# Turning the direction in which three products of a fused attention, gated convolution and channel mix kernel read their columns

## The chip, the cores and the metric

The kernel runs on one core of a Trainium2 chip. The metric is the device time of one execution in microseconds (us), from the profiler's clock of the chip. Several runs of the kernel before were timed. One further execution was profiled instruction by instruction, and all rows below come from it. PE is the matmul engine (PEld its weight loads), DVE the vector engine, ACT the scalar engine, POOL GpSimd, SP the engine that issues DMAs.

## What is computed

Batch 8, 8 heads, 576 positions, head size 64, so x has 8 × 576 rows of 512. Three stages follow one another:

```python
# linear attention, with softmax over features (q) and over positions (k)
kv = np.einsum('bhsd,bhse->bhde', k_s, v)
x = np.einsum('bhsd,bhde->bhse', q_s, kv)          # -> (8, 576, 512)
# gated causal convolution of 5 taps
gate = 1.0 / (1.0 + np.exp(-gate_pre))
y = gate * (x @ w_val) @ w_out
# channel mix with the position before
xk = mu_k * y + (1.0 - mu_k) * y_prev
xr = mu_r * y + (1.0 - mu_r) * y_prev
k = np.maximum(xk @ w_k, 0.0)                       # 512 -> 1024
v = k * k @ w_v                                     # 1024 -> 512
out = 1.0 / (1.0 + np.exp(-(xr @ w_r))) * v
```

## The kernel before, in words

The 4608 rows are cut into twelve tiles of T = 384 positions. Each tile i goes through five dense products, each with a name in the trace: pv (W_val, steps V), py (W_out, steps Y), racc (W_r, steps R), ph (W_k, steps H) and vacc (W_v, steps A). In pv, py and ph the weights are the stationary operand (128 × 128) and the activations are the moving operand, 384 columns; the output bank holds features by positions. In racc and vacc a slice of 128 positions of the activations is stationary (`part`, line 621) and a weight row of 512 columns moves; the output bank holds positions by features.

The first tile multiplies plain fp32 operands, one matmul call for each pair of operands (`left` has one member). From the second tile on, weights and activations are each split into a high and a low part of the type fp32r, and a product takes three passes: high by high and the two mixed ones. Both cases run through one helper, `passes` (lines 445 to 451), whose matmul call is line 449. So line 449 stands for all five dense products and for px, the product of q with the key-value sums; the output's name tells them apart in the trace.

The order of work is written out by hand: the list `FRONT` (lines 22 to 37) for the first two tiles with the loading and splitting of the weights, then for each tile the steps V, Y, R and an alternation of H and A, with the list `REST` saying which side steps (the attention of the next tile, the gates, the mixes) come after which step. Each engine's queue runs in that order. [...] ACT and DVE empty a bank after the last matmul of its group.

The change touches `passes` and its two kinds of callers: `product` (line 568), which pv, py and ph use from the second tile on, and the steps `r` (line 624) and `vacc` (line 646). The first tile's pv and py go through `row` (line 572).

Of the kernel before, what the change touches and what calls it, by code (L numbers as in the profile page):

```python
# [66 lines left out]
def tile_linear_attention_gated_conv_channel_mix(  # L67
# [15 lines left out]
    nc = tc.nc  # L83
    B, H, S, D = q.shape
    DM = H * D
# [3 lines left out]
    P = 128  # L89
    NC = DM // P  # L90
    NF = DFF // P
# [97 lines left out]
    def tap(c, t):  # L189
# [6 lines left out]


    HALF = ("wout", "wv")
    SHAPES = {"wval": (w_val, DM, DM), "wout": (w_out, DM, DM), "wr": (w_r, DM, DM), "wk": (w_k, DM, DFF), "wv": (w_v, DFF, DM)}
    CHUNKS = {  # L200
        f"{w}{x}": (w, at) for w, (_, rows, width) in SHAPES.items()
        for x, at in enumerate((kc, c0) for c0 in range(0, width, WC) for kc in range(rows // P))
# [4 lines left out]
    def place(dtype, name):  # L207
        return wts.tile([P, WC], dtype, tag="w", bufs=PLACES, name=name)

    def load_weight(n):  # L210
        w, (kc, c0) = CHUNKS[n]
        here = n in LEFT_WEIGHTS
        raw = raws[n] = (first if here else early).tile([P, WC, 2], U32, tag="raw", bufs=1 if here else 6, name="raw")
        nc.sync.dma_start(raw.rearrange("p n w -> p (n w)"), SHAPES[w][0][kc * P:(kc + 1) * P, 2 * c0:2 * (c0 + WC)])

# [5 lines left out]
    def open_upper():  # L221
        pool = ctx.enter_context(tc.tile_pool(name="upper", bufs=1))
        for w in ("wk", "wv"):
            _, rows, width = SHAPES[w]
            t = pool.tile([P, rows // P, width], F32R, name=f"{w}_hi")
            upper.update({(w, kc): t[:, kc, :] for kc in range(rows // P)})

    def split_weight(n):
# [9 lines left out]
        l = lower[at] = place(F32R, "lower")  # L238
        scale = 0.5 if w in HALF else 1.0
        nc.scalar.activation(h, t, AF.Copy, scale=scale)  # L240
        nc.vector.scalar_tensor_tensor(out=l, in0=t, scalar=scale, in1=f32(h), op0=ALU.mult, op1=ALU.subtract)

    def weight(i, w, kc, c0, n):

        at = w, (kc, c0 // WC * WC)
        o = c0 % WC
        if i == 0:
            return (whole[at][:, o:o + n],)
        return upper[w, kc][:, c0:c0 + n], lower[at][:, o:o + n]
# [192 lines left out]
        nc.vector.tensor_sub(pair[1], a, f32(pair[0]))  # L442
        return pair

    def passes(po, left, right, start, stop, turn=False):

        m = ((0, 0),) if len(left) == 1 else ((0, 0), (0, 1), (1, 0)) if turn else ((0, 0), (1, 0), (0, 1))
        for x, (a, b) in enumerate(m):
            nc.tensor.matmul(  # L449
                po, lhsT=left[a], rhs=right[b], start=start and x == 0, stop=stop and x == len(m) - 1  # L450
            )

    def padded(i, h, tag, bufs, name, pool=odd):

# [41 lines left out]
    def x_chunk(st, i, c):  # L496
        segs = segments(i)
        g = len(segs)
        px = ps_w.tile([P, 512], F32, tag="w", name="px")
        for o, n, b, s in segs:  # L500
            kv = (kvf[b],) if i < 2 else kvs[b % 2]
            passes(px[:, o:o + n], tuple(a[:, c, :] for a in kv), tuple(a[:, o:o + n] for a in st["q", c]), True, True)
        xv = padded(i, HALO, "xf", 2, "xf") if i else padded(i, HALO, "xf", NC, "xf", first)
        data = xv[:, :, HALO:]
        fill_past(i, xv, tail_x[:, c, :])
        nc.scalar.copy(data, px[:, :T].rearrange("p (g t) -> p g t", g=g))
        keep_tail(i, xv, tail_x[:, c, :])
        st["xv", c] = xv
        if i == 0:
            st["x", c] = (xv[:, 0, HALO:],)  # L510
            return
        xh, xl = st["x", c] = x_pair("x")
        gx = lambda a: a.rearrange("p (g t) -> p g t", g=g)
        nc.scalar.copy(gx(xh), data)
        nc.vector.tensor_sub(gx(xl), data, gx(f32(xh)))
# [38 lines left out]
    def main_steps(i, xs):  # L554
# [3 lines left out]
        st = {}  # L558
        gx = lambda a: a.rearrange("p (g t) -> p g t", g=g_n)

        def bank(pool, tag, name):
            return pool.tile([P, 512], F32, tag=tag, name=name)
# [4 lines left out]

        def product(po, w, at, acts):
            for c, a in enumerate(acts):
                passes(po, weight(i, w, c, at, P), a, c == 0, c == NC - 1)  # L570

        def row(po, w, c, a):

            for m in range(NC):
                passes(po[m][:, :T], weight(i, w, c, m * P, P), a, c == 0, c == NC - 1)

        def val(m):
            if i == 0:
                if m == 0:
                    st["pv"] = four("pv")  # L580
                row(st["pv"], "wval", m, xs["x", m])
                return
            pv = bank(ps_w, "w", "pv")
            product(pv[:, :T], "wval", m * P, [xs["x", c] for c in range(NC)])
            gated(m, pv)
# [8 lines left out]
        def y(c):  # L594
            if i == 0:
                if c == 0:
                    st["py"] = [bank(ps_w, "w", "py") if m < 2 else bank(ps_acc, "acc", "py") for m in range(NC)]
                row(st["py"], "wout", c, st["g", c])
                return
            py = bank(ps_w, "w", "py")  # L600
            product(py[:, :T], "wout", c * P, [st["g", m] for m in range(NC)])
            keep_y(c, py)
# [18 lines left out]
        def part(pair, t):  # L621
            return tuple(a[:, t * P:(t + 1) * P] for a in pair)

        def r(c):
            if c == 0:
                st["r"] = [bank(ps_acc, "acc", f"racc{t}") for t in range(NT)]
            for t in range(NT):
                passes(st["r"][t], part(st["xr", c], t), weight(i, "wr", c, 0, DM), c == 0, c == NC - 1, True)

        def rsig():  # L630
            for t in range(NT):
# [6 lines left out]
        def hid(f):  # L638
            ph = bank(ps_w, "w", "ph")
            product(ph[:, :T], "wk", f * P, [st["xk", c] for c in range(NC)])  # L640
            rf = one("k", 8, "rf") if i == 0 else scratch("rf")
            nc.scalar.activation(rf, ph[:, :T], AF.Relu)  # L642
            nc.scalar.activation(rf, rf, AF.Square)
            st["k", f] = (rf,) if i == 0 else split(rf, k_pair("k"))

        def vacc(fs, ts):

            if fs[0] == 0:
                st["v"] = [bank(ps_acc, "acc", f"vacc{t}") for t in range(NT)]
            for f in fs:  # L650
                for t in ts:
                    passes(st["v"][t], part(st["k", f], t), weight(i, "wv", f, 0, DM), f == 0, f == NF - 1, True)
            if fs[-1] == NF - 1 and len(ts) == NT:
                for t in ts:
                    finish(t)

        def finish(t):
            rs = st["rs", t]
            nc.vector.scalar_tensor_tensor(
                out=rs, in0=rs, scalar=1.0 if i else 0.0, in1=st["v"][t], op0=ALU.add, op1=ALU.mult  # L660
            )
            r0 = i * T + t * P
            nc.sync.dma_start(out[r0:r0 + P, :], rs)

        def last(t):

            vacc(range(NF - NT, NF), [t])
            finish(t)
# [6 lines left out]
        else:  # L675
            d += [("Z", t) for t in range(NT)]
        names = [("V", m) for m in range(NC)] + [("Y", c) for c in range(NC)] + [("R", c) for c in range(NC)] + d
        fns = {"V": val, "Y": y, "R": r, "H": hid, "A": lambda f: vacc([f], range(NT)), "Z": last}
        steps = {f"{n}{x}": lambda n=n, x=x: fns[n](x) for n, x in names}
        side = {"rsig": rsig}  # L680
# [127 lines left out]
```

## Time and profile before

| | |
|---|---|
| median of three runs | 812.14 us (810.77 to 812.4) |
| span of the profiled execution | 810.1 us |
| instructions in it | 12242 |
| PE busy | 798.3 us, 4578 matmul records |
| PEld busy | 701.2 us, 4578 weight loads |
| DVE busy | 564.5 us |
| ACT busy | 479.3 us |
| POOL busy | 59.2 us |
| DMA | 53.25 MB, mean 66 GB/s |

The span runs from the first instruction to the last; what lies around it makes up the rest of the time of a run. [...] A plain fp32 matmul leaves two records, an fp32r matmul one. The trace shows both types as f32; where the names hold `whole` the operands are plain fp32, where they hold `_hi`, `lower` or end in h or l they are fp32r.

### The profile page before, as it was taken

To read this page: it belongs to the slowest core of one execution; us is meant where nothing else is said; L and a number is where in the kernel's file an instruction comes from. 1 tells how busy PE (TensorE), PEld (TensorE's weight loads), DVE (VectorE), ACT (ScalarE), POOL (GpSimd) and SP (SyncE) were. 2 spreads that over 40 slices of the span, in tenths; PEclk is the share of its full clock that TensorE was granted. 3 is DMA by queue.
4 is the path that set the end of the run, shared out by engine and by line. 5 is a ranking of instruction groups with operands and counts; after the bars stand their busy time and mean duration, and the time that the engine had idled before them with its cause. 6 is when DMAs were issued, how large, how long until landed. Compare 5 with 4: busy or idle time off the path is not lost.

```text
span 810.1 us, 12242 instructions
## 1 busy us (share of the span) xinstructions
PE 798.3 (99%) x4578; PEld 701.2 (87%) x4578; DVE 564.5 (70%) x1016; ACT 479.3 (59%) x948; POOL 59.2 (7%) x224
## 2 busy tenths in 40 slices
PE   6999999999999999999999999999999999999998
PEld 5545588999999999989989999999999999998996
DVE  7999889976777577577758577577576747644611
ACT  4667678637746746655754763763764674664542
POOL 2130001000002001000000100100000100100000
PEclk9999999999999999999999999999999999999999
DMA  9786220132222102013041211211222010000001
GB/s 310 244 269 217 59 78 1 40 98 59 75 63 59 40 27 72 7 36 91 7 98 46 53 40 39 60 39 40 59 65 73 1 37 23 22 1 14 26 1 40
DMA packets 92537, 53.25 MB, mean 66 GB/s; under 512 B 74018, under 2 KB 84286, under 8 KB 92478
## 3 DMA queue, kind: packets, MB, share of 16 engines
q1 hardware_dynamic: 92432, 52.44, 22.3%
q8 instruction: 36, 0.59, 0.3%
q14 instruction: 23, 0.19, 0.1%
q10 hardware_dynamic: 46, 0.02, 0.0%
HBM read 43.02 MB, written 9.44 MB: 65 GB/s over the span
## 4 chain that ended last, share of the span: by engine, by line
PE 95%; DMA 2%; DVE 1%; ACT 1%; SPq 1%; issue 0%; ACTq 0%
PE ph L449 25%; PE vacc L449 25%; PE racc L449 12%; PE pv L449 12%; PE py L449 12%; PE px L449 4%; PE kvacc L347 2%; PE pq L476 2%; DMA raw<-in_moe_w_val_dram 1%; DMA raw<-in_moe_w_k_dram 1%; DVE gate L548 1%; DMA kt<-in_k_dram 1%; PE mx L333 0%; PE pmT L321 0%; SPq L303 0%; DVE whole L152 0%
## 5 line engine op out<-in xcount | busy, mean ns | idle before, releaser
L548 DVE SCALAR_TENSOR_TENSOR gate<-xf,cw,gate 128x384 f32<-128x384 f32 x192 | 117.2, 615 | 5.1 <-ACT gate L546 2.3
L449 PE MATMUL ph<-xkh,wk_hi 128*128 128x384 f32 x352 | 120.3, 342 | 0.0
L449 PE MATMUL ph<-xkl,wk_hi 128*128 128x384 f32 x352 | 118.3, 336 | 0.0
L449 PE MATMUL ph<-xkh,lower 128*128 128x384 f32 x352 | 118.1, 336 | 0.0
L642 ACT ACTIVATE rf<-ph 128x384 f32<-128x384 f32 x96 | 46.8, 488 | 99.0 <-PE ph L449 98.1
L449 PE MATMUL vacc<-wv_hi,kh 128*128 128x512 f32 x264 | 104.0, 394 | 0.0
L449 PE MATMUL vacc<-lower,kh 128*128 128x512 f32 x264 | 103.2, 391 | 0.0
L449 PE MATMUL vacc<-wv_hi,kl 128*128 128x512 f32 x264 | 103.1, 391 | 0.0
L442 DVE TENSOR_TENSOR kl<-rf,kh 128x384 fp32r<-128x384 f32 x88 | 48.9, 556 | 70.1 <-ACT kh L441 69.1
L616 DVE SCALAR_TENSOR_TENSOR xm<-yf,mus,xm 128x384 f32<-128x384 f32 x96 | 56.5, 614 | 24.2 <-ACT xm L615 23.7
L449 PEld LDWEIGHTS ph<-xkh,wk_hi 128*128 128x128 f32 x352 | 66.2, 188 | 2.0 <-ACT xkh L441 0.2
L449 PEld LDWEIGHTS ph<-xkh,lower 128*128 128x128 f32 x352 | 66.2, 188 | 1.9
L449 PEld LDWEIGHTS ph<-xkl,wk_hi 128*128 128x128 f32 x352 | 66.1, 188 | 0.0
L494 DVE TENSOR_TENSOR ql<-pq,qh 128x384 fp32r<-128x384 f32 x40 | 22.2, 556 | 62.5 <-ACT qh L493 62.5
L441 ACT CAST gh<-gf 128x384 fp32r<-128x384 f32 x44 | 22.5, 511 | 72.0 <-DVE gf L589 72.0
L449 PE MATMUL py<-gh,wout_hi 128*128 128x384 f32 x176 | 59.6, 343 | 0.0
L449 PE MATMUL pv<-xh,lower 128*128 128x384 f32 x176 | 59.5, 338 | 0.0
L449 PE MATMUL pv<-xh,wval_hi 128*128 128x384 f32 x176 | 59.5, 338 | 0.0
L449 PE MATMUL pv<-xl,wval_hi 128*128 128x384 f32 x176 | 59.3, 337 | 0.0
L449 PEld LDWEIGHTS vacc<-wv_hi,kl 128*128 128x128 f32 x264 | 49.5, 188 | 11.0 <-DVE kl L442 0.3
L449 PE MATMUL py<-gl,wout_hi 128*128 128x384 f32 x176 | 58.2, 339 | 0.0
L449 PE MATMUL py<-gh,lower 128*128 128x384 f32 x176 | 58.0, 338 | 0.0
(132 smaller groups left out, 1723.0 us busy)
## 6 DMA issues: line engine op xcount, KB each, us to landing
out_dram<-rs SPq DMA_DIRECT2D x36, 256.0 KB, 2.0
kt<-in_k_dram SPq DMA_DIRECT2D x16, 512.0 KB, 4.5
qt<-in_q_dram SPq DMA_DIRECT2D x29, 256.0 KB, 3.4
vt<-in_v_dram SPq DMA_DIRECT2D x56, 128.0 KB, 3.6
raw<-in_moe_w_k_dram SPq DMA_DIRECT2D x8, 512.0 KB, 5.5
raw<-in_moe_w_v_dram SPq DMA_DIRECT2D x8, 512.0 KB, 6.8
raw<-in_moe_w_val_dram SPq DMA_DIRECT2D x4, 512.0 KB, 6.3
raw<-in_moe_w_out_dram SPq DMA_DIRECT2D x4, 512.0 KB, 8.4
```

The source lines that it names most:

```text
L347: nc.tensor.matmul(acc[e * D:(e + 1) * D, x * VW:(x + 1) * VW], lhsT=kt[:, 2 * x + e, s, :], rhs=st["v"][:, 2 * x + e, s, :], start=(s == ...
L441: nc.scalar.copy(pair[0], a)
L442: nc.vector.tensor_sub(pair[1], a, f32(pair[0]))
L449: nc.tensor.matmul(po, lhsT=left[a], rhs=right[b], start=start and x == 0, stop=stop and x == len(m) - 1)
L476: nc.tensor.transpose(pq[:, t * P:(t + 1) * P], qt[:, t, 2 * c:2 * c + 2, :].rearrange("p h d -> p (h d)"), f32(ident))
L494: nc.vector.tensor_sub(ql, pq[:, :T], f32(qh))
L548: nc.vector.scalar_tensor_tensor(out=gx(gate), in0=xv[:, :, HALO - sh:HALO - sh + L], scalar=tap(c, HALO - sh), in1=gx(gate), op0=ALU.mult ...
L616: nc.vector.scalar_tensor_tensor(out=gx(xf), in0=yv[:, :, 1:], scalar=mu[:, c:c + 1], in1=gx(xf), op0=ALU.mult, op1=ALU.add)
L642: nc.scalar.activation(rf, ph[:, :T], AF.Relu)
```

## The change

Where a product is listed in `BACK`, the moving operand and the output of its matmuls are both given as views with the last dimension turned round (`[:, ::-1]`). That is W_val, W_r and W_k, wherever the operands come in two parts; with one part (the first tile) nothing changes. The stationary operand is given as before. The call for W_v carries the new argument too, but W_v isn't listed.

```diff
     HALF = ("wout", "wv")
+    BACK = ("wval", "wr", "wk")
...
-    def passes(po, left, right, start, stop, turn=False):
+    def passes(po, left, right, start, stop, turn=False, back=False):
 
         m = ((0, 0),) if len(left) == 1 else ((0, 0), (0, 1), (1, 0)) if turn else ((0, 0), (1, 0), (0, 1))
+        back = back and len(left) > 1
+        o = po[:, ::-1] if back else po
         for x, (a, b) in enumerate(m):
-            nc.tensor.matmul(
-                po, lhsT=left[a], rhs=right[b], start=start and x == 0, stop=stop and x == len(m) - 1
-            )
+            r = right[b][:, ::-1] if back else right[b]
+            nc.tensor.matmul(o, lhsT=left[a], rhs=r, start=start and x == 0, stop=stop and x == len(m) - 1)
...
-                passes(po, weight(i, w, c, at, P), a, c == 0, c == NC - 1)
+                passes(po, weight(i, w, c, at, P), a, c == 0, c == NC - 1, back=w in BACK)
...
-                passes(st["r"][t], part(st["xr", c], t), weight(i, "wr", c, 0, DM), c == 0, c == NC - 1, True)
+                passes(st["r"][t], part(st["xr", c], t), weight(i, "wr", c, 0, DM), c == 0, c == NC - 1, True, "wr" in BACK)
...
-                    passes(st["v"][t], part(st["k", f], t), weight(i, "wv", f, 0, DM), f == 0, f == NF - 1, True)
+                    passes(st["v"][t], part(st["k", f], t), weight(i, "wv", f, 0, DM), f == 0, f == NF - 1, True, "wv" in BACK)
```

## Rows read from the trace of the kernel before

**Rows 1.** The page's totals: engine, busy us, share of the span, instructions.

```profile
PE 798.3 (99%) x4578; PEld 701.2 (87%) x4578; DVE 564.5 (70%) x1016; ACT 479.3 (59%) x948; POOL 59.2 (7%) x224
```

**Rows 2.** The page's 40 equal slices, PE's busy tenths and granted clock's.

```profile
PE   6999999999999999999999999999999999999998
...
PEclk9999999999999999999999999999999999999999
```

**Rows 3.** The page's chain that ended last, by engine and by line.

```profile
PE 95%; DMA 2%; DVE 1%; ACT 1%; SPq 1%; issue 0%; ACTq 0%
PE ph L449 25%; PE vacc L449 25%; PE racc L449 12%; PE pv L449 12%; PE py L449 12%; PE px L449 4%; PE kvacc L347 2%; PE pq L476 2%; DMA raw<-in_moe_w_val_dram 1%; DMA raw<-in_moe_w_k_dram 1%; DVE gate L548 1%; DMA kt<-in_k_dram 1%; PE mx L333 0%; PE pmT L321 0%; SPq L303 0%; DVE whole L152 0%
```

**Rows 4.** Waits of PE: for whom, us in total, times, longest us.

```profile
PE heat L738 <- DVE ident L158: 3.3, 1, 3.3
PE pmT L321 <- DVE pm L314: 2.5, 1, 2.5
PE racc L449 <- ACT yf L607: 0.7, 1, 0.7
PE pq L476 <- ACT q L488: 0.7, 1, 0.7
PE pmT L321 <- ACT q L488: 0.6, 1, 0.6
PE px L449 <- ACT q L488: 0.2, 1, 0.2
```

**Rows 5.** Timeline inside one ph group: start us, us, engine, line, what.

```profile
407.47 0.34 PE L449 MATMUL ph<-xkh,lower 128*128 128x384 f32 x1
407.47 0.19 PEld L449 LDWEIGHTS ph<-xkl,wk_hi 128*128 128x128 f32 x1
407.64 0.34 PE L449 MATMUL ph<-xkl,wk_hi 128*128 128x384 f32 x1
407.65 0.19 PEld L449 LDWEIGHTS ph<-xkh,wk_hi 128*128 128x128 f32 x1
407.82 0.34 PE L449 MATMUL ph<-xkh,wk_hi 128*128 128x384 f32 x1
```

**Rows 6.** Pieces of the chain in order of time, fp32r: start us, us, matmuls.

```profile
198.32 2.08 PE ph L449 x12
...
747.97 8.34 PE pv L449 x48
...
764.78 8.17 PE racc L449 x36
```

**Rows 7.** Pieces of the same chain in the first tile, plain fp32.

```profile
81.40 2.58 PE ph L449 x8
85.78 2.58 PE vacc L449 x6
```

**Rows 8.** Groups by shape, PE, one pass of each: count, busy us, mean ns.

```profile
L449 PE MATMUL ph<-xkh,wk_hi 128*128 128x384 f32 x352 | 120.3, 342 | 0.0
...
L449 PE MATMUL pv<-xh,wval_hi 128*128 128x384 f32 x176 | 59.5, 338 | 0.0
...
L449 PE MATMUL racc<-wr_hi,xrh 128*128 128x512 f32 x132 | 51.4, 389 | 0.0
```

**Rows 9.** Groups by shape, weight loads: fp32, a plain run, one column repeated.

```profile
L449 PEld LDWEIGHTS ph<-xm,whole 128*128 128x128 f32 x64 | 11.9, 190 | 8.5 <-issue 1.9
...
L321 PEld LDWEIGHTS pmT<-ident,pm 128*128 128x128 f32 x32 | 4.3, 140 | 4.8 <-DVE pm L314 2.7 <-ACT q L488 0.8 <-issue 0.7
L333 PEld LDWEIGHTS mx<-ident,m 128*128 128x128 f32 x32 | 4.2, 141 | 2.1 <-DVE m L323 1.2
```

**Rows 10.** Groups by shape, ACT: copies out of PSUM, plain and in steps.

```profile
L486 ACT COPY q<-pq 128x384 f32<-128x384 f32 x4 | 1.9, 481 | 1.1 <-PE pq L476 1.1
L488 ACT COPY q<-pq 128x384 f32<-128x384 f32 x4 | 1.8, 475 | 2.4 <-PE pq L476 2.4
```

## The prediction

> **What bounds the kernel now.** I read the views in this order: the page's totals, its slices, the chain, the waits of the matmul engine, then single matmuls. The totals [rows 1] give PE 798.3 us of a span of 810.1, DVE 564.5, ACT 479.3. A busy PE alone proves little, since a matmul's record overlaps the next one's. [...] The chain that ended last [rows 3] is 95% PE, and nearly all of it is line 449, the one matmul call in `passes`: ph 25%, racc 12% and pv 12% belong to the products that are changed, vacc 25% and py 12% to those that are not. PE's waits are 8.0 us in six pieces [rows 4], the two longest 3.3 and 2.5 us, and none is in a product that is changed, except 0.7 us in the first tile's racc, which the change leaves alone. So what a matmul of line 449 costs more or less lands in the time one for one, as long as PE stays the engine that is late.
>
> What one matmul costs is read from the distance between starts, not from its record. The record of a 384-column matmul lasts 0.34 us, but the next starts 0.17 or 0.18 us later [rows 5]. The pieces of the chain give it exactly [rows 6]: 48 of pv in 8.34 us, 173.8 ns each; 12 of ph in 2.08 us, 173.3; 36 of racc in 8.17 us, 226.9. The two widths split this into a part per column and a fixed part. [...] The first tile multiplies in plain fp32, with two records per matmul, and there the chain [rows 7] shows 8 of ph in 2.58 us, 322.5 ns each, and 6 of vacc at 512 columns in 2.58 us, 430: 107.5 ns per 128 columns, 0.84 ns each, and nothing left over as a fixed part. [...]
>
> **The change part by part.** First, how many matmuls turn around. `back` is dropped where `left` has one member, and that is the first tile. Of the others the groups by shape [rows 8] hold 176 of pv, 352 of ph and 132 of racc for one of three passes, and the other two passes have as many: 528 + 1056 = 1584 at 384 columns and 396 at 512, 1980 in all. At today's distances they take 1584 × 173.5 = 274.8 us and 396 × 226.9 = 89.9 us, 364.7 us together, 45% of the span. py, vacc, px, the transposes and all of the first tile run as before.
>
> Second, what is not touched. No instruction is added or taken away, no tile is larger, no DMA moves, nothing passes a queue. The weight loads read `left`, which isn't turned. Each output element lands at its old address, because operand and output are turned alike: column 383 is read first and written to place 383. ACT and DVE read the bank after the last matmul of the group, so they wait for the same event as now. A column's sum is added up in the same order of passes. No wait is added and no buffer comes free at another point of the order.
>
> Third, the one thing that is touched: the step along the columns is −1 in SBUF and in PSUM. No matmul of the trace reads or writes so, and its price has to be bounded. For the cost per column one end is zero: the same columns, still neighbours. The far end is the slower of the rates that the engine shows, the first tile's: 322.5 instead of 173.5 ns at 384 columns and 430 instead of 226.9 at 512, so 1584 × 149.0 = 236.0 us and 396 × 203.1 = 80.4 us, together 316 us. [...] The fixed part can go both ways: at best it vanishes, as in the fp32 rows, −1980 × 13.3 ns = −26.3 us; as the other end I take that it doubles, +26.3 us.
>
> Which end is nearer? Three rows show an access that isn't a plain ascending run from an even place, and in none is it dearer. The weight load of mx reads one column over and over (step 0, from `to_broadcast` in line 333) and takes 141 ns, that of pmT reads 128 columns in a row and takes 140 [rows 9]. ACT's copy out of the bank in line 488 reads in steps of 128 places (the `rearrange` there) and takes 475 ns, the plain copy in line 486 takes 481 [rows 10]. [...] I take zero for both parts, and keep both ends.
>
> [...]
>
> **The sum.** The profiled execution: 810.1 us, +0 per column, +0 fixed, 810.1 us after. The median of the runs shown is 812.14 us, 2.0 us above that span, which lies around it and isn't touched. Forecast: 812.1 us, no change. The zero isn't hidden behind other work: PE is the path, so any nanosecond per matmul would show, 2.0 us for each. DVE at 564.5 us and ACT at 479.3 have room on either side: neither becomes the bound if PE lost 26 us, and if PE took longer their work would only be covered better.
>
> **The rivals.**
> - *Half rate.* [...] Time: 812.1 + 316 = 1128 us, and 1150 if the fixed 13.3 ns come on top (1980 × 11 to 13 ns). [...] Chance 0.20. [...]
> - *A dearer start.* A matmul that begins at the far end pays more before its first column or after its last. Price up to 13.3 ns each, as above: 812.1 to 838 us, with the middle at 825. It decides from 0.8 ns per matmul (1.6 us over 1980). For it: the fixed 13.3 ns exist and no row tells what they are. Against it: they are alike at 384 and 512 columns and in pv, ph and racc, though these read from quite different tiles. Chance 0.14.
> - *A cheaper start.* The fixed part is a meeting of the next weight load and the moving columns, both read upward now; the loads start with the matmul before them and last 0.19 us [rows 5], so the two do run side by side. Turning one of them might spare some of it, at most 26.3 us: 786 to 812 us. Against it: a load as long, 190 ns [rows 9], stands beside the fp32 matmuls, where nothing is left over, and the distance is the same for all weights. Chance 0.13.
> - *It doesn't do what it says*: the turned view is made into a plain one when the program is built. Then the times are those of no change; it is counted there, with 0.03.
>
> **How the numbers follow.** No change 0.53 (with the 0.03 above), half rate 0.20, dearer start 0.14, cheaper start 0.13. A measurement of this kernel can tell about 0.2% (1.6 us) from no change, so faster is 0.13, same 0.53, slower 0.20 + 0.14 = 0.34. The range that leaves out the half rate alone holds 0.80: from 812.1 − 26.3 = 786 to 812.1 + 26.3 = 838 us. The likeliest case's own range is 810.5 to 813.8.
>
> **What would show it.** If I'm right, 48 of pv still take 8.3 us in the chain, 36 of racc 8.2 and 12 of ph 2.1, and the span stays at 810. At half rate, the starts of turned matmuls stand 0.32 us (384) and 0.43 us (512) apart while py and vacc keep 0.17 and 0.23. If only the start is dearer or cheaper, pv and racc change by the same nanoseconds at both widths. If pv and ph change and racc doesn't, it hangs on what is read (activations there, weights in racc), not on the step as such. The forecast is wrong if any distance between starts moves by over 0.8 ns on the mean of the 1980, or if py or vacc move though they weren't edited.

## The result: 820.8 us, 1.07% slower, with the profile after

The changed kernel takes 820.84 us (median, 819.93 to 821.29) beside 812.25 us of the kernel before: a ratio of 1.0107, 95% interval 1.0093 to 1.0122. The time lies inside the range, but the forecast was no change, and the kernel is slower by 8.6 us, with an interval that leaves no change far outside.

The page's totals and chain of the changed kernel answer to [rows 1] and [rows 3]. Line 449 is line 453 now.

```profile
PE 806.1 (99%) x4578; PEld 706.3 (86%) x4578; DVE 565.2 (69%) x1016; ACT 479.8 (59%) x948; POOL 59.2 (7%) x224
...
PEclk9999999999999999999999999999999999999999
...
PE ph L453 25%; PE vacc L453 25%; PE racc L453 12%; PE pv L453 12%; PE py L453 11%; PE px L453 3%; PE kvacc L348 3%; PE pq L478 2%; DMA raw<-in_moe_w_k_dram 1%; DVE gate L550 1%; PE heat L740 1%; PE pmT L322 1%; PE mx L334 0%; DVE whole L152 0%; DVE raw L151 0%; DVE gf L591 0%
```

PE has 7.8 us more of busy time and as many records, DVE and ACT have what they had, and the granted clock is as in [rows 2], 9 tenths or more in all slices, 0.997 in the mean before and 1.000 after. The five products make up 85% of the chain, 86 before, and no other entry moves by more than 1%. The span is 817.9 us, 7.8 above that of before. The pieces of the chain (start us, us, what) that answer to [rows 6] and [rows 7] say where the time went:

```profile
81.05 2.58 PE ph L453 x8
85.42 2.58 PE vacc L453 x6
...
138.26 2.12 PE ph L453 x12
...
692.58 8.53 PE pv L453 x48
701.11 8.47 PE py L453 x48
709.58 8.40 PE racc L453 x36
...
748.17 4.12 PE vacc L453 x18
```

The last of these answers to this piece of the kernel before:

```profile
741.27 4.09 PE vacc L449 x18
```

A matmul of pv takes 8.53 / 48 = 177.7 ns in place of 173.8, of ph 176.7 in place of 173.3, of racc 233.3 in place of 226.9. The pieces of ph are short, so 0.01 us in one of them is 0.8 ns; the mean over all distances inside groups of ph in the two traces is 176.5 in place of 173.4. Adding up the time from each start to the next over the whole trace, by product, gives 3.1 us more in ph, 2.0 in pv and 2.4 in racc, 7.5 together. py, which wasn't turned, keeps its 8.47 us, and the plain fp32 matmuls of the first tile keep theirs. But vacc, which wasn't turned either, does not stay as it was: its mean distance rises from 228.8 to 230.0 ns, 1.0 us over its 792 matmuls. With 0.6 us less in py and px and small changes elsewhere, the sum over PE is 7.7 us, beside 7.8 in the span.

### The profile page after: what moved, and what is told of

The parts are those of the page before. It is cut to its first block, busy times and chain, and to the rows that moved or that the text cites. A ratio compares the mean times of both kernels' runs of the same rounds, so it can differ in the third digit from the quotient of the medians.

```text
span 817.9 us, 12248 instructions
## 1 busy us (share of the span) xinstructions
PE 806.1 (99%) x4578; PEld 706.3 (86%) x4578; DVE 565.2 (69%) x1016; ACT 479.8 (59%) x948; POOL 59.2 (7%) x224
## 4 chain that ended last, share of the span: by engine, by line
PE 96%; DVE 1%; DMA 1%; ACT 1%; issue 0%; ACTq 0%
PE ph L453 25%; PE vacc L453 25%; PE racc L453 12%; PE pv L453 12%; PE py L453 11%; PE px L453 3%; PE kvacc L348 3%; PE pq L478 2%; DMA raw<-in_moe_w_k_dram 1%; DVE gate L550 1%; PE heat L740 1%; PE pmT L322 1%; PE mx L334 0%; DVE whole L152 0%; DVE raw L151 0%; DVE gf L591 0%
```

## Experiments

Each kernel is compared with the kernel before, run beside it on the same chip. The kernels that hold many forms at once, called ladders below, ran once each and are read from their traces. "Distance" is the time from one matmul's start to the next one's. Most views are the same kind of row: the 36 matmuls of racc in one tile as a piece of the chain, which took 8.17 us before (226.9 ns each) and 8.40 after (233.3).

### Reading or writing: e1 and e2

e1 keeps the downward read and writes upward:

```diff
-            o = po[:, ::-1] if back else po
+            o = po
```

e2 keeps the downward write and reads upward:

```diff
-            r = right[b][:, ::-1] if back else right[b]
+            r = right[b]
```

> The moving operand of pv, ph and racc is read from the last column to the first, and the output is written upward, so the columns of these products come out mirrored and the kernel computes something else; counts and shapes are those of the changed kernel. Theory A (the price is in reading downward): the time of the changed kernel, 820.8 us, with mean distances of 177.8 ns in pv, 176.7 in ph and 233.4 in racc. Theory B (the price is in writing downward): the time of the kernel before, 812.2 us, with 173.5, 173.3 and 226.9 ns. Theory C (each side pays a part): between, and this run and the next add up to 8.6 us.

> The other half: operand read upward, output of pv, ph and racc written downward, again with mirrored columns. Theory A (reading): 812.2 us and the distances of the kernel before. Theory B (writing): 820.8 us and 177.8, 176.7 and 233.4 ns. Theory C: the rest of the 8.6 us.

Reading downward and writing upward: 820.77 us, ratio 1.0104 (1.0087 to 1.0121). Reading upward and writing downward: 812.28 us, ratio 0.9998 (0.9988 to 1.0007). One tile of each, e1 first:

```profile
692.92 8.53 PE pv L453 x48
701.45 8.47 PE py L453 x48
709.92 8.40 PE racc L453 x36
```

```profile
686.79 8.32 PE pv L453 x48
695.11 8.47 PE py L453 x48
703.58 8.17 PE racc L453 x36
```

Theory A holds: the pieces are those of the changed kernel in e1 and those of the kernel before in e2. The whole price is in reading the moving operand downward; writing to PSUM downward cost nothing.

### One pass alone, and all products: e3 and e4

e3 turns the second pass of three alone:

```diff
+            down = back and x == 1
+            o = po[:, ::-1] if down else po
+            r = right[b][:, ::-1] if down else right[b]
```

e4 turns all five products:

```diff
-    BACK = ("wval", "wr", "wk")
+    BACK = ("wval", "wout", "wr", "wk", "wv")
```

> Operand and output are turned in the second of the three passes alone, so the sums are those of the reference. Theory D (a fixed price for each downward matmul, wherever it stands): a third of the 8.6 us, 815.1 us, and the extra nanoseconds sit at the middle pass. Theory E (what counts is where one matmul ends and the next begins: up then down starts at the column just left): the price at the two turns differs from that of down after down; under 812.2 us if a turn spares the jump back to the other end of the row, over 820.8 us if adding to a column that was written a moment ago has to wait.

> W_out and W_v are turned as well. Theory D (fixed price by product shape): py has the shape of pv and ph and should gain 3.3 to 4.3 ns on 528 matmuls, 1.7 to 2.3 us, and vacc the shape of racc, 6.5 ns on 792, 5.1 us: 827.6 to 828.2 us. Theory F (the price comes of two directions next to each other, since py and vacc stay upward between the turned products): with one direction throughout it goes away, and the time is 812.2 us or near it.

e3 takes 818.46 us (1.0061 to 1.0091): a third of the matmuls, three quarters of the price. Neither theory gave that. In racc a piece of 36 takes 8.25 us, a third of the way from 8.17 to 8.40, as a fixed price would have it; in pv the 48 take 8.48, most of the way from 8.34 to 8.53, and in ph the mean distance is 176.5 ns, as with all three passes down. vacc, which isn't turned, rises to 230.9 ns. e4 takes 824.77 us (1.0134 to 1.0164), 3.9 us above the changed kernel where theory D wanted 6.8 to 7.4 and theory F a fall. The 48 of py rise from 8.47 to 8.59 us, 2.5 ns each, and vacc's mean distance from 230.0 in the changed kernel (228.8 before) to 233.4 ns. vacc had less to lose: it stood above 226.9 already. So there is no fixed price per downward matmul; what one pays depends on the matmuls around it, and matmuls that aren't turned can pay too.

### Ladders of widths, passes and starts: e5, e6 and e8

From here on one kernel holds many forms: a table `HOW` says for each product and tile how `passes` slices and turns, and the trace is read tile by tile. Shown is the core of e5.

```diff
         for x, (a, b) in enumerate(m):
-            nc.tensor.matmul(
-                po, lhsT=left[a], rhs=right[b], start=start and x == 0, stop=stop and x == len(m) - 1
-            )
+            first, end = start and x == 0, stop and x == len(m) - 1
+            l, r, o = left[a], right[b], po
+            if how and not first and not end:
+                lo, hi, down, held = how
+                l, r, o = l[:, 0:held], r[:, lo:hi], o[0:held, lo:hi]
+                if down:
+                    r, o = r[:, ::-1], o[:, ::-1]
+            nc.tensor.matmul(o, lhsT=l, rhs=r, start=first, stop=end)
```

e6 turns only the passes that `HOW` lists, in the first tile too; e8 is e5 with other columns and an output written upward.

> A ladder in one kernel: each tile of 384 positions runs racc, pv and ph in another form, so one trace holds all. racc: tile 2 down at 512 columns, 3 and 4 up and down at 384, 5 and 6 at 256, 7 up over columns 2 to 511, 8 down over 0 to 509, 9 and 10 up and down with 64 stationary columns, 11 down at 448. pv: tile 2 down at 384, 3 and 4 up and down at 320, 5 and 6 at 256, 7 and 8 with 64 stationary columns, 9 and 10 down and up at 352, 11 down over 0 to 381. ph: tile 2 down at 384, 3 and 4 down and up at 368, 5 down at 380, 6 at 376, 7 and 8 up and down over 16 to 383, 9 up from 2, 10 up from 14, 11 down over 0 to 381. The first and last matmul of each group stay whole and upward; parts of the products are left out. What counts are distances between starts, down minus up. Theory G (a fixed price at the start of a downward read): racc plus 6.4 ns at all widths, pv plus 4. Theory H (a price per column): racc plus 6.4, 5.6, 4.8 and 3.2 ns at 512, 448, 384, 256, pv from 4.1 at 384 to 2.7 at 256. Theory I (moving columns and weight load get in each other's way): with 64 stationary columns upward 512 takes 220 ns in place of 226.9, and the price of down falls to about 3. Theory J (what counts is the address on which a read begins): upward reads from 2 or 14 pay as the downward ones do, and downward ones from 510, 380, 376 or 368 differ from those from 384 or 512.

> A second ladder, operand and output turned alike, so the sums stay those of the reference. In pv, racc and ph, by tile: 0 all downward in plain fp32; 2 downward in the first and third pass; 3 none; 4 first pass alone; 5 second alone; 6 third alone; 7 first and second; 8 every other matmul; 9 all; 10 second and third. Theory D (a fixed price for each downward matmul): three distances of racc take 680.5 ns with none, plus 6.4 for each downward pass, and pv and ph 521 ns plus 3.3 to 4.3 for each. Theory E (turns matter): what a pass costs depends on its neighbours; by the run with the middle pass alone pv would take 529 with one downward pass, and the first or third pass alone would give the same 529; every other matmul would cost nearly as much as all. For tile 0: if the price is a wait in a stream that has no slack, fp32 at half the rate has slack and keeps 322.5 ns at 384 and 430 at 512 columns; if it is a start that nothing hides, 326 to 329 and 436.

> One width, other starting columns. racc with 448 columns: upward from column 0 (tile 1), 2, 4, 8, 16 and 32 (tiles 2 to 6), downward over the 448 columns from column 0, 2, 4, 8 and 16 (tiles 7 to 11). ph the same with 352 columns. pv by width, up and down: 368 (tiles 2, 3), 336, 304, 288, 272 (tiles 10, 11). The other columns are left out except in the first and last matmul of a group. Theory K (pieces of 16 columns): upward from 16 and 32 as from 0, 200.0 ns in racc; upward from 2, 4 and 8 dearer by the price of one more piece or by that of all pieces; downward from 16 as from 0, 205 ns. Theory M (start address alone): each start has its own price, upward and downward, with no order. The law of the first ladder, 0.026 ns for each column beyond 256, gives pv down minus up 2.9 ns at 368, 2.1 at 336, 1.2 at 304, 0.8 at 288 and 0.4 at 272.

Mean distances in ns, up and down, worked out from the starts in the traces, between matmuls of the same width (e5, where marked e8; whole rows upward from the kernel before for racc and from tile 1 of e5 for pv):

| read | up | down |
|---|---|---|
| racc, 512 columns | 227.0 | 233.6 |
| racc, columns 2 to 511 up, 0 to 509 down | 234.2 | 233.4 |
| racc, 448 columns (e8) | 203.5 | 205.9 |
| racc, 384 | 174.0 | 177.1 |
| racc, 256 | 119.4 | 118.1 |
| racc, 512, 64 columns held | 230.1 | 233.4 |
| pv, 384 | 173.6 | 177.5 |
| pv, 368 (e8) | 166.8 | 167.5 |
| pv, 336 (e8) | 154.8 | 153.1 |
| pv, 304 (e8) | 138.2 | 139.9 |
| pv, 256 | 118.5 | 118.1 |
| pv, 384, 64 columns held | 172.9 | 175.9 |

After e5 alone a law offered itself, 0.026 ns for each column beyond 256. e8 was its test, and it fell: 2.9, 2.1 and 1.2 ns were to stand between up and down at 368, 336 and 304 columns, measured were 0.7, −1.7 and 1.7. An upward read isn't always where a line through the whole rows of [rows 6] puts it either, 0.417 ns per column ((226.9 − 173.5) / 128) and 13.3 ns more: the first 384 columns of racc come near it, 174.0 for 173.5, but 448 columns would take 200 ns and take 203.5 from column 0, 206.2 from 2, 202.3 from 4, 205.5 from 8, 200.8 from 16 and 203.1 from 32. Theories G and H fail at 256 and 336 columns, where down isn't the dearer one; theory J fails in ph, where 382 columns from column 2 upward take 173.6 ns and 382 downward 176.9. What the ladder leaves is that width and start count for an upward read too: in racc one that begins two columns later takes 234.2 ns, where that line gives 226.1 for 510 columns, and so pays as much as a downward one.

Theory I is half borne out. Holding 64 columns shortens the record of a weight load from 188 to 134 ns, but an upward matmul of racc doesn't come down to 220 ns, it takes 230.1. What turning costs does fall, to 3.3 ns in racc and 3.0 in pv, near the 3 that was expected, though in racc only because the upward read got dearer. Groups by shape of e5's loads (count, busy us, mean ns):

```profile
L488 PEld LDWEIGHTS racc<-wr_hi,xrh 128*128 128x128 f32 x114 | 21.4, 188 | 3.0 <-ACT xrh L473 0.3
...
L488 PEld LDWEIGHTS racc<-wr_hi,xrh 128*64 128x64 f32 x18 | 2.4, 134 | 1.6
```

e6 answers two questions. Its first tile turns plain fp32, and the pieces of the chain show ph as in [rows 7]; racc of tiles 2 to 5, 9 and 11 follow (first and third pass down, none, first alone, second alone; all; none):

```profile
81.34 2.58 PE ph L488 x8
...
190.13 8.39 PE racc L488 x36
255.95 8.17 PE racc L488 x36
320.12 8.32 PE racc L488 x36
384.18 8.25 PE racc L488 x36
...
644.37 8.40 PE racc L488 x36
...
769.41 8.17 PE racc L488 x36
```

In plain fp32, at 322.5 / 384 = 0.84 ns per column and record, reading downward costs nothing: 322.5 ns. And one downward pass of three costs 0.15 us of the 0.23 if it is the first, 0.08 if it is the second, and 0.20 if it is the third (8.37 us); the first two together, at 8.45 us, cost more than all three. The neighbours count, as e3 said.

### Which step downward costs: e7 and e9

```diff
+    def read(a, how):
+
+        lo, hi, block, outer, inner = how
+        a = a[:, lo:hi]
+        if block:
+            a = a.rearrange("p (a b) -> p a b", b=block)
+            a = a[:, ::-1, :] if outer else a
+            return a[:, :, ::-1] if inner else a
+        return a[:, ::-1] if inner else a
```

e9 adds "every h-th group" and "swapped pairs" to it by a `rearrange` with three factors.

> The row is cut into blocks and only the order of the read is changed, the output is written upward, so columns come out permuted. Counted in racc (512 columns), pv and ph (384). Tile 2 all downward; 3 to 7: blocks taken from the last to the first, upward inside, with blocks of half the row, 64, 16, 4 and 2 columns; 8 to 11: blocks taken upward, downward inside, with blocks of 16, 4, 64 and half the row. The first and last matmul of each group stay upward and whole. [...] Theory K (a read is done in pieces of some columns, and what costs is the step from a piece to the one below): blocks of half the row cost nothing, blocks of 64 a fourth of the price or less, blocks of 16 and smaller the price of all downward, and blocks taken upward with downward reads inside 16 or 4 cost nothing. Theory L (what costs is each step of -1, wherever it is): blocks of 16, 4 and 2 taken down, upward inside, cost less the larger they are, and 16 or 4 downward inside cost as all downward. Theory M (what counts is only at which address a read begins and ends): half the row swapped already costs 6.6 ns in racc.

> A third ladder of read orders, racc with 512 columns, pv and ph with 384, output written upward, so columns come out permuted. Tiles 2, 3, 4: blocks of 8, 32 and 128 columns taken downward, upward inside; 5, 6, 7: blocks of 8, 32 and 128 taken upward, downward inside; 8 and 9: every second group of 4 or of 16 columns, then the others; 10: every fourth group of 4; 11: groups of 4 swapped in pairs. [...] Theory N (what counts is that the next group of 4 isn't the one above): every second group, every fourth group and swapped pairs cost as much as all downward, 233.3. If the direction is what counts, every second and every fourth group upward cost nothing.

racc of e7, tiles 2 to 11 in order: all downward; blocks of 256, 64, 16, 4 and 2 taken downward, upward inside; blocks of 16, 4, 64 and 256 taken upward, downward inside.

```profile
190.56 8.41 PE racc L496 x36
256.55 8.17 PE racc L496 x36
320.60 8.17 PE racc L496 x36
384.14 8.39 PE racc L496 x36
450.31 8.41 PE racc L496 x36
515.13 8.41 PE racc L496 x36
580.26 9.43 PE racc L496 x36
649.12 8.17 PE racc L496 x36
...
711.45 8.40 PE racc L496 x36
...
773.78 8.40 PE racc L496 x36
```

The tile with blocks of 4 taken upward, downward inside, is at 8.17 us: three of its four steps are −1 and it pays nothing. With blocks of 64 taken downward, upward inside, also 8.17; with blocks of 16 or less, the full price. So the direction of single columns within a group of 4 doesn't count, and it isn't only where a read begins or ends, since half the row swapped is free (against theories L and M). What counts is the order of the groups of 4. Blocks of 16 with downward reads inside are the dearest at 9.43 us, against theory K. e9 brought no single rule either: blocks of 8 and 32 taken downward give 8.40 and 8.32 us and 128 gives 8.17, while orders that go only upward, every second group of 4 or of 16, give 8.33 and 8.57, so jumps upward cost as well. One order was cheaper than reading straight on: every fourth group of 4, racc 8.12 us and pv 7.97 for its 48 (166 ns each).

```profile
693.90 7.97 PE pv L500 x48
...
710.34 8.12 PE racc L500 x36
```

### The same in whole kernels: e10 and e11

The diff is that of e10; in e11 the slice is `[:, :, ::-1]`.

```diff
+        def fours(a):
+            return a.rearrange("p (a b) -> p a b", b=4)[:, ::-1, :]
-        o = po[:, ::-1] if back else po
+        o = fours(po) if back else po
...
-            r = right[b][:, ::-1] if back else right[b]
+            r = fours(right[b]) if back else right[b]
```

> The changed kernel with the rows of pv, ph and racc taken in groups of four columns from the last group to the first, upward inside a group, operand and output alike, so the sums are those of the reference. If the price is in going down from group to group, and the direction of single columns costs nothing, the time is that of the changed kernel, 820.8 us; if it is in the step of -1 from column to column, 812.2 us or a fourth of the 8.6 us above it, 814.3.

> The counterpart: groups of four columns taken from the first to the last, downward inside a group, operand and output alike, sums as in the reference. Three of four steps along a row are -1. If going down from group to group is the price, the time is that of the kernel before, 812.2 us; if the step of -1 from column to column is, three fourths or all of the 8.6 us, 818.6 to 820.8.

Groups downward, columns upward inside: 820.46 us, 1.0101 (1.0086 to 1.0116). Groups upward, columns downward inside: 812.32 us, 0.9997 (0.9988 to 1.0007). The step of −1 isn't the price; going down from group to group is.

### Does the read meet the weight load: e12

```diff
+    def shift(w, i, at, room):
+
+        by = HOW.get((w, i), (0, False))[0]
+        return at + by if at % room + P + by <= room else at - by
+
+    def moved(w, i, at):
+        return shift(w, i, at, WC)
...
-                passes(po, weight(i, w, c, at, P), a, c == 0, c == NC - 1)
+                passes(po, weight(i, w, c, moved(w, i, at), P), a, c == 0, c == NC - 1, how=HOW.get((w, i)))
...
-        def part(pair, t):
-            return tuple(a[:, t * P:(t + 1) * P] for a in pair)
+        def part(pair, t, w):
+            at = shift(w, i, t * P, T)
+            return tuple(a[:, at:at + P] for a in pair)
```

> The weight load begins some columns further on (or back, where the tile ends) in the five products, so other columns are held and the sums differ; the moving operand is as before. Tiles 2 to 6: upward reads with the stationary slice moved by 4, 8, 12, 16 and 32 columns; tile 7 downward, not moved; 8 to 11 downward, moved by 4, 8, 16 and 32. [...] Theory Q (only the order in which the moving read visits its groups of 4 columns counts): shifts change nothing, 226.7 up and 233.3 down in racc, 173.5 and 177.8 in pv.

In the upward tiles the moving read stays as it was, and only the place from which the stationary slices are loaded moves, in all five products at once. racc, tiles 2 to 6 upward with the slice moved by 4, 8, 12, 16 and 32 columns, then tile 7 downward, not moved, and tile 11 downward, moved by 32:

```profile
191.12 8.16 PE racc L510 x36
256.68 8.40 PE racc L510 x36
321.49 8.34 PE racc L510 x36
385.53 8.34 PE racc L510 x36
451.54 8.36 PE racc L510 x36
516.43 8.40 PE racc L510 x36
...
773.44 8.52 PE racc L510 x36
```

A load that begins 8 columns further on costs an upward read 0.23 us in 36, in the mean as much as turning costs, though not one address of the moving read has changed; and the loads' records keep their 188 ns. It need not be the same delay: the single distances go from 229 to 239 ns with the shift, and from 233 to 234 when turned. In pv a shift of 4 columns gives 176.0 ns in place of 173.4, shifts of 8 and 12 give 174. So theory Q is out: the distance hangs on the place of the stationary slice as well. It isn't a price of its own that is added to that of turning either: downward reads take 8.41, 8.40, 8.40 and 8.52 us with shifts of 4, 8, 16 and 32, so that turning costs 0.25 us more at 4 and nothing at 8. That the moving read and the load of the next weights meet in SBUF (theory P of e14 and e15) is the author's guess; no trace shows a meeting, and no run moves the slice of one product alone. Downward, no shift brings back 8.17.

### Other orders, and a faster kernel: e13, e14 and e15

```diff
+            r = right[b]
+            if how:
+                r = r.rearrange("p (a h b) -> p h a b", b=how[0], h=how[1])
```

> Read orders that stay upward but jump, in all five products, output written upward, so columns come out permuted. Groups of b columns, every h-th of them, then the next ones: tile 2: b 4, h 4; 3: 4, 8; 4: 4, 16; 5: 4, 32; 6: 8, 2; 7: 8, 4; 8: 8, 8; 9: 16, 4; 10: 2, 8; 11: 4, 2. The ladder before gave 164.7 ns in pv, 172.3 in ph and 224.3 in racc for b 4, h 4, against 173.5, 173.4 and 226.7 upward. Theory R (jumps of 64 bytes keep the read in one part of SBUF that the weight load visits rarely): h 8, 16 and 32 with b 4 do the same, 160 to 166 ns in pv, and py, which has the alignment of ph, stays near 172. Theory S (a bare read order has a price of its own, and the gain of pv is a phase between neighbours): h 8, 16 and 32 differ from h 4 without an order, and some are above 173.5.

racc of e13: every fourth group of 4, every eighth, every fourth group of 8, and groups of 2 with every eighth taken.

```profile
190.14 8.18 PE racc L504 x36
256.60 8.87 PE racc L504 x36
...
537.24 7.95 PE racc L504 x36
...
747.80 15.52 PE racc L504 x36
```

Every eighth group of 4 is dearer, not as good as every fourth, so theory R is out. pv with every fourth group takes 170.1 ns, where e9 had 166: still under 173.5, but not the same number, as theory S had it. In the last row, with only two columns of a group of 4 at a time, the matmul takes 15.52 / 36 = 431 ns, as long as a record of the fp32 rows at 512 columns [rows 7]. That is 256 visits to a group at 1.68 ns, and four columns of a whole row take 4 × 0.417 = 1.67 ns. An estimate from these two numbers is that a visit to a group costs the same for two columns as for four; no run shows the read itself, and whole groups visited in wider jumps are dearer as well (every eighth, 8.87 us).

e14 uses the ladders' best orders in whole kernels, operand and output alike; e15 does it for W_r alone (`ORDER = {'wr': (8, 4)}`).

```diff
+    ORDER = {'wval': (4, 4), 'wout': (4, 4), 'wk': (4, 4), 'wr': (8, 4)}
...
+        def visit(a):
+            if w not in ORDER or len(left) == 1:
+                return a
+            b, h = ORDER[w]
+            return a.rearrange("p (a h b) -> p h a b", b=b, h=h)
```

> The kernel before, with W_val, W_out and W_k read (and written) upward in groups of 4 columns, every fourth group, and W_r in groups of 8, every fourth, so the sums are those of the reference. Theory P (the read of the moving operand and the weight load meet in SBUF, and the order of the read sets how often): the ladder's distances, 170.1 ns in pv, 172.0 in py, 172.7 in ph and 219.9 in racc, against 173.4, 173.4, 173.2 and 226.7, give 528 x 3.3 + 528 x 1.4 + 1056 x 0.5 + 396 x 6.8 = 5.7 us, so 806.5 us. Theory S (the gain was a phase of that one tile, or writing in such an order costs what reading gains): 812.2 us or more.

> The same for W_r alone, groups of 8 columns, every fourth. Theory P: 396 x 6.8 ns = 2.7 us less, 809.5 us, racc at 220 ns in every tile. Theory S: 812.2 us, and racc at 220 ns in some tiles alone.

e15 takes 809.70 us, 0.9966 (0.9953 to 0.9979) of the kernel before: faster than both kernels of this case, and as theory P had it from racc alone. Its racc takes 7.92 or 7.93 us in all ten tiles that have it in one piece. e14 takes 811.56 us, 0.9985 (0.9976 to 0.9995), 1.2 us under the kernel before beside it and a fifth of what was expected. One row of e15, then two of e14:

```profile
761.31 7.92 PE racc L456 x36
```

```profile
188.91 8.37 PE racc L456 x36
...
763.07 7.99 PE racc L456 x36
```

pv gains its part (8.18 us for 48), but the same racc with the same order takes 8.27 to 8.37 us in the first eight of those tiles and 7.99 in the last two, which have no attention for a next tile among their steps. vacc, whose order is as before, takes 230.3 ns in place of 228.8 and loses about another 1 us. The instructions of racc are the same in e14 and e15, and in the same tiles they take 8.27 us or more in the one and 7.92 or 7.93 in the other; what differs is the order in which the products around them read. So what went before a run of matmuls counts for the rhythm they fall into. That is theory S for that part.

## Why the prediction was wrong, point by point

**What bounds the kernel** was right. PE stayed the path, the extra nanoseconds landed one for one (7.7 us by the starts of PE, 7.8 in the span, 8.6 in the time), DVE and ACT had room, no wait moved.

**How many matmuls** was right: 1584 and 396, and the first tile untouched. That py, vacc and px run as before was not quite: vacc, not edited, lost 1.2 ns each, 1.0 us, one of the signs that the prediction had named.

**The step that failed** is "which end is nearer". It took zero for both parts, the one per column and the fixed one, because the rows with a step other than 1 cost nothing: a weight load with step 0, 141 ns beside 140, and ACT's copy in steps of 128, 475 ns beside 481 [rows 9, 10]. One is the loading of weights and the other is another engine; neither is a moving read. What the runs showed in its place: a moving read that goes down the row group by group, four columns each, costs 3 to 4 ns per matmul at 384 columns and 6.4 at 512, all of it on the reading side (e1, e2, e10, e11). The rows used also lack what may have mattered, a stream without slack: on the same engine the first tile, at 0.84 ns per column and record where fp32r has 0.417, reads downward for nothing (322.5 ns, e6). That fits, but fp32 differs in more than its rate, so the missing slack is the author's guess and isn't shown to be the cause.

**The bounds** were too coarse in the middle. Per column they knew only the two rates of the trace, 0.417 and 0.84 ns, and the truth was 3 to 6.4 ns per matmul, 2 to 3% of it. The far end also took the distance of a record for that of a matmul: plain fp32 leaves two records per matmul, so a whole one takes 645 ns at 384 columns, not 322.5. Half the rate did come in e13, 431 ns, but for another order than the changed one. The range stands on 1980 × 13.3 ns, and no run shows these 13.3 ns as a cost of their own: they are what the line through [rows 6] leaves, and other upward reads stood 6.4 ns (racc in e15, 220.0 ns), 16.6 ns (448 columns in e8, 203.5 ns) and 21.4 ns (racc from column 2 in e5, 234.2 ns) above 0.417 ns per column.

**The rivals.** The measured time, 820.8, lies in "a dearer start", 812 to 838, which had a chance of 0.14; its price per matmul, up to 13.3 ns, was 3 to 6.4. That the number fell into it is luck, since its mechanism isn't the one: its own sign, the same nanoseconds at both widths, didn't come, and a row read in two halves upward, downward inside each, begins in the middle and pays in full (8.40 us, e7). "A cheaper start" had the right partner, if theory P holds, and the wrong sign: the upward read of whole rows beside the load as it stood was a cheap case already, and most other orders and places that were tried are dearer (e8, e12, e13), though not all (e15). Its "Against it", that the distance is the same for all weights, was read as independence; a shift of 8 columns undid it, 8.40 us in place of 8.17 (e12). "Half rate", 1128 us, didn't come, and the order inside a group of four is free: 812.32 us (e11).

**What stays open.** Why a load of half the length doesn't make an upward matmul shorter (e5), what rule says which order and place are cheap, in which order a load reads its own columns, and why a rhythm, once taken, lasts for a whole run of matmuls (e14). That downward reads of groups cost is shown, 820.46 us (e10); by what path the place of the load counts is not. No run here separates these.

## What to carry to other kernels

Where matmuls stand start to start at 0.417 ns per column, as in [rows 6], the order in which the moving operand is read and the place of the stationary operand beside it can be part of the cost: the same 512 columns took 220 to 431 ns here. It is read from the distance between starts. Writing downward (812.28 us) and plain fp32 matmuls (322.5 ns) didn't care here. Bound an unknown access by rows of the same kind of read at the same rate; rows of another engine (475 ns beside 481), or of the same engine at half the rate (322.5 ns up and down), showed nothing of this price.

## What was unexpected

- The order within a group of 4 columns is free, the order of the groups isn't: 820.5 us with groups taken downward, 812.3 with columns taken downward inside them.
- A shift of the stationary slices by 8 columns costs an upward read of racc 6.4 ns on 226.9, with no address of the moving read changed.
- Reading two columns at a time, each pair from another group of four, takes nearly twice the time: 431 ns in place of 226.9 for 512 columns.
- Matmuls that weren't turned paid too: vacc went from 228.8 to 230.0 ns.
- The fixed 13.3 ns per fp32r matmul aren't fixed: racc in groups of 8, every fourth, takes 7.92 / 36 = 220.0 ns, 6.4 above the 213.6 that 512 columns take at 0.417 ns each.
